# A convolution and SwiGLU kernel: bursts of the down projection one step later, the copy behind the product, and x and out on the software DMA queue

## The chip, the core and the metric

The kernel runs on one core of one Trainium2 chip. The metric is the device time of one execution in microseconds; the kernel before has a median of 895.02 us over 10 runs (894.46 to 896.08).

## The reference

x has 8 sequences of 4096 tokens with 192 channels. Stage one is a causal convolution with 7 taps: the 192 channels are 8 heads of 24, and each head has one softmax-normalised kernel of 7 weights. Stage two is a SwiGLU feed-forward block with an inner width of 1536 on the 32768 tokens that come out. All is in float32.

```python
w = softmax(weight, axis=-1)                       # 8 heads x 7 taps
x_pad = np.concatenate([zeros(B, 6, D), x], axis=1)
conv = np.einsum('hk,bskhg->bshg', w, windows(x_pad)).reshape(B * S, D)
g, v = conv @ moe_w_gate, conv @ moe_w_val         # 192 -> 1536
out = (g / (1 + np.exp(-g)) * v) @ moe_w_out       # 1536 -> 192
```

## The kernel before

The tokens are worked off in blocks of 512 (TB); two blocks make a unit of 1024 tokens (UB, UT), so there are 64 blocks and 32 units. The inner width is cut into 12 chunks of 128 (NCH). One pass of the main loop (L374) is a step g: one chunk of one block. A unit has 24 steps, and s is the step within its unit (L376).

In a step TensorE makes the gate product of chunk g and the value product of chunk g - 1 (emit_gv, L277), both over 192 channels in three pieces of 64 rows. The gate uses the upper half of the array's rows and the value the lower half, so the two run side by side. ScalarE puts SiLU on the gate (emit_silu, L292), and VectorE multiplies it with the value product from PSUM and writes h as fp16 (emit_h, L297). gate and val have two PSUM buffers each (ppool, L70); a val buffer is free again when its product h is made.

The down projection runs in bursts of three chunks (TR, L49): emit_f2 (L302) takes three chunks of h in two halves, in two successive steps out of three. F2_LAG (L50) says how many steps behind the gate it runs: 4. Behind the last burst of a block, emit_store (L337) copies the two accumulators to SBUF, one on ScalarE (L340), one on VectorE (L341); this stands ahead of emit_h in the step's order (L407 to L412). The 384 KB of a block go to `out` on SP's queue, four steps into the next block (L429).

The third step of three has no burst, and four of these eight gaps in a unit take the convolution of the next unit (emit_conv, L218, at s = 0, 3, 6, 9): small matmuls of band matrices (toep) with x as fp16, into two PSUM tiles. Since the two halves of the array swap banks between bursts, a relay stands between a burst and the next: a nop on GpSimd's queue that waits for the last matmul of a burst and that the first matmul of the next burst waits for (emit_relay, L209).

The convolved tokens have to be transposed. ScalarE copies them to SBUF as fp16 (emit_conv_out, L243, at s = 3, 4, 9, 10), GpSimd repeats the first 64 channels behind the others (emit_dup, L251), SP writes each block to DRAM (emit_to_dram, L257, at s = 11, 12), 57 partitions by 9 rows of 512 bytes, and SP reads it back by three transposing DMAs for each block (emit_transpose, L269, one a step from s = 16). The result xq of the first block of the next unit is needed by that unit's step 0, piece by piece.

x itself comes in on SP's queue as float32 (emit_fetch, L88, at s = 6 for the unit after the next: 64 x 9, 64 x 8 and 62 rows of 768 bytes), and GpSimd casts it in three parts (emit_x_cast, L104, at s = 14 to 16).

The order on all five engines is the written one (manual_schedule, L108): each engine works off its queue in the order in which the code emits, and waits only for data and buffers. Ahead of the main loop stand the loads (x of unit 0, all weights in two parts, x of unit 1, all on SP's queue), the making of the band matrices on VectorE, the convolution of unit 0, the casts of the weights in four parts, and the way through DRAM of blocks 0 and 1.

## Time and profile before

| What | Value |
|---|---|
| median of 10 runs | 895.02 us (894.46 to 896.08) |
| the profiled execution | 895.45 us |
| its span in the profile | 893.7 us, TensorE clock 0.999 |
| TensorE matmuls busy | 836.2 us (94%) |
| VectorE, ScalarE, GpSimd busy | 559.9, 547.8, 89.8 us |
| first gate matmul | 40.8 us |
| start of units 1, 3, 4 and 31 | 68.2, 121.56, 147.81 and 861.4 us |
| moved by DMA | 100.8 MB, 113 GB/s on average |
| issued by SP's queue | 63 out stores, 63 writes of xc, 189 transposes, 104 x loads |

The span is the time from the first to the last instruction; the execution's own time lies 1.75 us above it. In the profile PE stands for TensorE, PEld for its weight loads, DVE for VectorE, ACT for ScalarE, POOL for GpSimd and SPq for SP's queue, which issues DMAs. A row of the timeline has its start and its length in us; what stands in brackets at its end is the idle time of the engine before it and what ended that. In the list of waits, the numbers behind a pair are the sum in us, the count and the longest. A matmul's recorded length overlaps with the next one's, so steps are measured from start to start.

### The profile page before, as it was taken

The numbers are of one execution on the slowest core, as the hardware profiler recorded it, in microseconds if no ns is written. First come the engines' busy times: TensorE is split into PE (matmuls) and PEld (weight loads), VectorE is DVE, ScalarE is ACT, GpSimd is POOL, SyncE is SP. The second block draws the span as 40 slices with busy tenths as digits, with TensorE's granted clock in tenths as the row PEclk, the third lists the DMA queues.
The fourth block names the chain that finished last, engine by engine and source line by source line (L and its number), as shares of the span: only waits on it lengthen the run. The fifth ranks groups of instructions, "written<-read, shape, count | busy, mean of one in ns | idle before, by whom it ended". The sixth has DMA issues, their size and how long they took to land.

```text
span 893.7 us, 28535 instructions
## 1 busy us (share of the span) xinstructions
PE 836.2 (94%) x11764; PEld 595.5 (67%) x11764; DVE 559.9 (63%) x865; ACT 547.8 (61%) x970; POOL 89.8 (10%) x148
## 2 busy tenths in 40 slices
PE   1199999999999999999999999999999999999997
PEld 0176776677676677676667777667767667777764
DVE  5066666666666666666666666666666666666665
ACT  3166666666666666666656666666666666666654
POOL 2111011011001011001011101101100101110000
PEclk9999999999999999999999999999999999999999
DMA  9554665454565464555555456545556645555351
GB/s 180 108 108 98 124 130 115 98 124 100 118 124 125 89 130 103 112 125 128 110 107 118 96 125 127 123 94 123 114 105 125 132 102 111 122 101 120 86 95 37
DMA packets 211843, 100.80 MB, mean 113 GB/s; under 512 B 107056, under 2 KB 210944, under 8 KB 211712
## 3 DMA queue, kind: packets, MB, share of 16 engines
q1 hardware_dynamic: 209292, 98.12, 52.4%
q8 instruction: 92, 1.51, 0.7%
q10 hardware_dynamic: 2420, 0.85, 0.6%
q14 instruction: 39, 0.32, 0.1%
HBM read 31.79 MB, written 41.98 MB: 83 GB/s over the span
## 4 chain that ended last, share of the span: by engine, by line
PE 84%; DMA 7%; DVE 6%; SPq 2%; issue 1%; ACT 1%; DVEq 0%; POOLq 0%
PE acc L312 28%; PE val L284 26%; PE gate L284 24%; PE cps L233 5%; DMA xq<-xc 4%; DMA xc<-stage 3%; DVE h L299 2%; DVE o_sb L341 2%; SPq L273 1%; DVE band L180 1%; SPq L346 0%; DMA wraw<-in_weight_dram 0%; ACT stage L245 0%; ACT sig L294 0%; ACT toep L188 0%
## 5 line engine op out<-in xcount | busy, mean ns | idle before, releaser
L299 DVE TENSOR_TENSOR h<-sig,val 128x512 f16<-128x512 f16 x768 | 518.1, 687 | 271.0 <-PE val L284 233.1
L294 ACT ACTIVATE sig<-gate 128x512 f16<-128x512 f32 x768 | 458.8, 597 | 308.3 <-PE gate L284 186.5
L284 PE MATMUL gate<-xq,w_sb 64*128 64x512 f16 x2304 | 614.2, 377 | 26.8 <-DMA xq<-xc 26.4
L284 PE MATMUL val<-xq,w_sb 64*128 64x512 f16 x2304 | 608.2, 377 | 12.8 <-DVE h L299 12.5
L284 PEld LDWEIGHTS <-w_sb 64*128 64x128 f16 x4608 | 287.9, 94 | 176.3 <-issue 70.4
L312 PE MATMUL acc<-wo_sb,h 64*128 64x192 f16 x6120 | 402.5, 243 | 0.5 <-DVE h L299 0.5
L312 PEld LDWEIGHTS <-h 64*128 64x128 f16 x6120 | 328.6, 94 | 84.5 <-DVE h L299 1.0
L233 PE MATMUL cps<-x,toep 64*128 64x216 f16 x1024 | 82.9, 257 | 13.2 <-POOL x L106 12.0
L106 POOL CAST x<-x 128x576 f16<-128x576 f32 x96 | 62.9, 674 | 310.2 <-PE acc L312 298.1
L233 PEld LDWEIGHTS <-toep 64*128 64x128 f16 x1024 | 63.1, 95 | 32.3 <-DVE toep L187 10.1
L341 DVE COPY o_sb<-acc 128x384 f32<-128x384 f32 x64 | 35.7, 558 | 56.5 <-PE acc L312 55.9
L245 ACT ACTIVATE stage<-cps 128x432 f16<-128x432 f32 x128 | 67.1, 526 | 2.0 <-PE cps L233 2.0
L253 POOL COPY stage<-stage 128x576 f16<-128x576 f16 x32 | 21.4, 669 | 428.3 <-PE acc L312 398.2
L340 ACT COPY o_sb<-acc 128x384 f32<-128x384 f32 x64 | 30.7, 479 | 1.7 <-PE acc L328 1.7
L193 ACT CAST w_sb<-w_st 128x1152 f16<-128x1152 f32 x4 | 4.4, 1150 | 20.2 <-issue 20.1
L180 DVE COPY_PREDICATED band<-mask,whl 128x228 int32<-128x228 int32 x14 | 6.9, 495 | 0.4
L188 ACT COPY toep<-band 64x456 f16<-64x456 f16 x2 | 1.2, 578 | 7.0 <-DVE band L180 7.0
L194 POOL CAST wo_sb<-wo_st 128x576 f16<-128x576 f32 x4 | 2.6, 670 | 13.0 <-DMA wo_st<-in_moe_w_out_dram 13.0
L92 POOL MEMSET x<- 6x192 f32 x8 | 2.0, 248 | 1.3 <-PE cps L233 1.3
L158 ACT ACT_TABLE_LOAD x1 | 1.3, 1283 | 0.7 <-PEq L447 0.7
L158 ACT ACTIVATE wexp<-wexp 128x56 f32<-128x56 f32 x1 | 0.2, 249 | 2.1 <-DVE wexp L155 2.1
L328 PE MATMUL acc<-wo_sb,h 128*128 128x192 f16 x12 | 1.3, 248 | 0.1
(21 smaller groups left out, 8.2 us busy)
## 6 DMA issues: line engine op xcount, KB each, us to landing
out_dram<-o_sb SPq DMA_DIRECT2D x63, 384.0 KB
xc<-stage SPq DMA_DIRECT2D x63, 256.5 KB
x<-in_x_dram SPq DMA_DIRECT2D x40, 384.0 KB
x<-in_x_dram SPq DMA_DIRECT2D x24, 432.0 KB
xq<-xc SPq DMA_TRANSPOSE x189
x<-in_x_dram SPq DMA_DIRECT2D x32, 46.5 KB
w_st<-in_moe_w_gate_dram SPq DMA_DIRECT2D x2, 576.0 KB
wo_st<-in_moe_w_out_dram SPq DMA_DIRECT2D x2, 576.0 KB
```

The source lines that it names most:

```text
L106: nc.gpsimd.tensor_copy(x16s[u % 2][:, gs, :], x32s[u % 2][:, gs, :])
L180: nc.vector.copy_predicated(band_w[:, hs], masks[k].unsqueeze(1).to_broadcast([P, 4, G]), whl_w[:, hs, k : k + 1].to_broadcast([P, 4, G]),)
L233: mm = nc.tensor.matmul(conv["ps"][a][:, :, e, :], toep[lo : lo + Q, h, c, :], x16[lo : lo + Q, :, h * grp : (h + 1) * grp], start=(phase ...
L245: nc.scalar.mul(conv[u][:, :, d0 : d0 + 2 * grp], conv["ps"][a].rearrange("p g e d -> p g (e d)"), 1.0 / SCALE,)
L253: nc.gpsimd.tensor_copy(conv[u][:, :, D:XD], conv[u][:, :, 0:Q])
L273: queue.dma_start_transpose(out=xqs[b][:, q, :], in_=drs[b][0:TB, q * Q : q * Q + P])
L284: last_mm[0] = nc.tensor.matmul(ps, w_r[lo : lo + Q, q, ts(j, P)], xq[lo : lo + Q, q, :], start=(q == 0), stop=(q == NQ - 1),)
L294: nc.scalar.activation(sj, ps, AF.Silu)
L299: nc.vector.tensor_tensor(hj, sj, ps, op=ALU.mult)
L312: mm = nc.tensor.matmul(acc[a][:, i, :], hlist[j][lo : lo + Q, ts(2 * a + i, P)], wo_r[lo : lo + Q, j, :], start=(j == 0 and half == 0 and ...
L340: nc.scalar.copy(o_sb[:, 0:2, :], acc[0])
L341: nc.vector.tensor_copy(o_sb[:, 2:4, :], acc[1])
```

## The change

F2_LAG becomes 5, so each burst moves by one step, and h gets a tenth buffer. The convolution moves with the gaps, to s = 1, 4, 7, 10 (in unit 0 to s = 7, 10, 13, 16), and with it its copies, the repeat (dup) and the two writes to DRAM (s = 12, 13; in unit 0 s = 18, 19); the transposes start at s = 16 as before (in unit 0 at s = 18). The copy of the accumulators stands behind emit_h. The store to `out` goes to GpSimd's DMA queue, one step later, except for the last block's. The fetch of x is cut into its DMAs, which GpSimd's queue issues one a step from s = 10, the upper partitions first; the casts move to s = 19 to 21. At the start, x of unit 0 is loaded by SP (lower half of the partitions) and ScalarE's queue (upper half), the weights come in quarters, and the last quarter and x of unit 1 are issued behind the transposes of block 0. The last quarter's cast stands in step 6 of unit 0, and the casts of unit 1's x in its steps 4 to 6. The write and the transposes of block 0 go from ScalarE's queue to SP's.

```diff
@@ -47,7 +47,7 @@
     UT = UB * TB
     XD = D + Q
     TR = 3
-    F2_LAG = TR + 1
+    F2_LAG = TR + 2
     SCALE = 1024.0
 
     assert D == NQ * Q and NQ == 3 and UB == 2 and UG * G >= TB
@@ -85,21 +85,27 @@
             tensor=x_flat.tensor, offset=t * D, ap=[[D, rows], [G * D, n], [1, D]]
         )
 
-    def emit_fetch(u):
+    def fetches(u, lower=nc.gpsimd, upper=nc.gpsimd):
+
         x32 = x32s[u % 2]
         t0 = u * UT - pad
+        tb = t0 + TB
+        tl = tb + (UG - 1) * G
+        todo = [
+            (upper, x32[Q:P, 0 : UG - 1, :], windows(tb, Q, UG - 1)),
+            (upper, x32[Q : Q + last_rows, UG - 1, :], x_flat[tl : tl + last_rows, :]),
+        ]
         if u % upb == 0:
             nc.gpsimd.memset(x32[0:pad, 0, :], 0.0)
-            nc.sync.dma_start(out=x32[pad:Q, 0, :], in_=x_flat[t0 + pad : t0 + Q, :])
-            nc.sync.dma_start(out=x32[0:Q, 1:UG, :], in_=windows(t0 + G, Q, UG - 1))
+            todo.append((lower, x32[pad:Q, 0, :], x_flat[t0 + pad : t0 + Q, :]))
+            todo.append((lower, x32[0:Q, 1:UG, :], windows(t0 + G, Q, UG - 1)))
         else:
-            nc.sync.dma_start(out=x32[0:Q, :, :], in_=windows(t0, Q, UG))
-        tb = t0 + TB
-        nc.sync.dma_start(out=x32[Q:P, 0 : UG - 1, :], in_=windows(tb, Q, UG - 1))
-        tl = tb + (UG - 1) * G
-        nc.sync.dma_start(
-            out=x32[Q : Q + last_rows, UG - 1, :], in_=x_flat[tl : tl + last_rows, :]
-        )
+            todo.append((lower, x32[0:Q, :, :], windows(t0, Q, UG)))
+        return todo
+
+    def emit_fetch(todo):
+        queue, dst, src = todo.pop(0)
+        queue.dma_start(out=dst, in_=src)
 
     def emit_x_cast(u, i):
         gs = slice(i * UG // 3, (i + 1) * UG // 3)
@@ -113,7 +119,9 @@
     nc.sync.dma_start(
         out=wraw, in_=bass.AP(tensor=weight.tensor, offset=0, ap=[[0, P], [K, H], [1, K]])
     )
-    emit_fetch(0)
+    first = fetches(0, nc.sync, nc.scalar)
+    while first:
+        emit_fetch(first)
 
 
     w_st = wpool.tile([P, NQ, Dff], fp32, tag="w_st", name="w_st")
@@ -124,15 +132,17 @@
     wg_v = moe_w_gate.rearrange("(q p) f -> p q f", p=Q)
     wv_v = moe_w_val.rearrange("(q p) f -> p q f", p=Q)
     wo_v = moe_w_out.rearrange("(c p) d -> p c d", p=P)
-    for f in range(0, Dff, 2 * FS):
-        fs = slice(f, f + 2 * FS)
-        cs = slice(f // P, (f + 2 * FS) // P)
+
+    def emit_weight_load(i):
+        fs = slice(i * FS, (i + 1) * FS)
+        cs = slice(i * FS // P, (i + 1) * FS // P)
         nc.sync.dma_start(out=w_st[0:Q, :, fs], in_=wg_v[:, :, fs])
         nc.sync.dma_start(out=w_st[Q:P, 0 : NQ - 1, fs], in_=wv_v[:, 1:NQ, fs])
         nc.sync.dma_start(out=w_st[Q:P, NQ - 1, fs], in_=wv_v[:, 0, fs])
         nc.sync.dma_start(out=wo_st[:, cs, :], in_=wo_v[:, cs, :])
-    if n_units > 1:
-        emit_fetch(1)
+
+    for i in range(3):
+        emit_weight_load(i)
 
 
     diag = const_pool.tile([P, G], i32, tag="diag", name="diag")
@@ -254,11 +264,11 @@
 
     drs = {}
 
-    def emit_to_dram(b, queue=nc.sync):
+    def emit_to_dram(b):
 
         u, i = divmod(b, UB)
         dr = tc.dram_tile([UG * G, XD], fp16, name=f"xc{b}")
-        queue.dma_start(
+        nc.sync.dma_start(
             out=dr.rearrange("(g r) d -> r g d", r=G),
             in_=conv[u][i * Q : i * Q + G],
         )
@@ -266,11 +276,11 @@
 
     xqs = {}
 
-    def emit_transpose(b, q, queue=nc.sync):
+    def emit_transpose(b, q):
 
         if q == 0:
             xqs[b] = xpool.tile([P, NQ, TB], fp16, tag="xq", name="xq")
-        queue.dma_start_transpose(
+        nc.sync.dma_start_transpose(
             out=xqs[b][:, q, :], in_=drs[b][0:TB, q * Q : q * Q + P]
         )
 
@@ -295,7 +305,7 @@
         return sj
 
     def emit_h(sj, ps, hlist):
-        hj = hpool.tile([P, TB], fp16, tag="h", name="h", bufs=9)
+        hj = hpool.tile([P, TB], fp16, tag="h", name="h", bufs=10)
         nc.vector.tensor_tensor(hj, sj, ps, op=ALU.mult)
         hlist.append(hj)
 
@@ -343,7 +353,7 @@
         if b == n_blocks - 1:
             nc.scalar.dma_start(out=o_v[:, 0:2], in_=o_sb[:, 0:2])
             return lambda: nc.sync.dma_start(out=o_v[:, 2:4], in_=o_sb[:, 2:4])
-        return lambda: nc.sync.dma_start(out=o_v, in_=o_sb)
+        return lambda: nc.gpsimd.dma_start(out=o_v, in_=o_sb)
 
     for fill in range(2):
         for phase in range(2):
@@ -353,19 +363,19 @@
             emit_conv_out(0, fill, a)
         if fill == 0:
             emit_dup(0)
+    emit_to_dram(0)
     emit_weight_cast(0)
-    emit_to_dram(0, nc.scalar)
     emit_weight_cast(1)
     for q in range(NQ):
-        emit_transpose(0, q, nc.scalar)
+        emit_transpose(0, q)
+    first = fetches(1, nc.sync, nc.sync) if n_units > 1 else []
+    while first:
+        emit_fetch(first)
+    emit_weight_load(3)
+    emit_weight_cast(2)
     emit_to_dram(1)
-    for i in range(2, 4):
-        emit_weight_cast(i)
     for q in range(NQ):
         emit_transpose(1, q)
-    if n_units > 1:
-        for i in range(3):
-            emit_x_cast(1, i)
 
     hlists, accs, stores = {}, {}, []
     ns = NCH * UB
@@ -399,34 +409,43 @@
             if half < 2 and not tail:
                 emit_f2(half, range(t * TR, (t + 1) * TR), accs[fb], hlists[fb])
                 burst = True
-        if more and s in (0, 3, 6, 9):
-            emit_conv(u + 1, s // 6, s // 3 % 2)
+
+        c0 = 7 if u == 0 else 1
+        if more and s in range(c0, c0 + 12, 3):
+            emit_conv(u + 1, (s - c0) // 6, (s - c0) // 3 % 2)
             burst = True
-        if burst and live:
+        if burst:
             emit_relay()
+        if val is not None:
+            emit_h(sil.pop(g - 1), val[0], hlists[vb])
         if g >= F2_LAG and fj == NCH - 2:
             if tail:
                 emit_f2_full(range(t * TR, NCH), accs[fb], hlists[fb])
             stores.append(emit_store(fb, accs.pop(fb)))
-        if val is not None:
-            emit_h(sil.pop(g - 1), val[0], hlists[vb])
         if g >= F2_LAG and fj == NCH - 1:
             del hlists[fb], xqs[fb]
         if more:
-            if s in (3, 4, 9, 10):
-                emit_conv_out(u + 1, s // 6, s % 3)
-            if s == 5:
+            if s in (c0 + 3, c0 + 4, c0 + 9, c0 + 10):
+                emit_conv_out(u + 1, (s - c0) // 6, (s - c0) % 3)
+            if s == c0 + 5:
                 emit_dup(u + 1)
+            if u == 0 and 4 <= s < 7:
+                emit_x_cast(1, s - 4)
             if u + 2 < n_units:
-                if s == 6:
-                    emit_fetch(u + 2)
-                if 14 <= s < 17:
-                    emit_x_cast(u + 2, s - 14)
-            if s in (11, 12):
-                emit_to_dram((u + 1) * UB + s - 11)
-            if 16 <= s < 16 + UB * NQ:
-                emit_transpose((u + 1) * UB + (s - 16) // NQ, (s - 16) % NQ)
-        if s % NCH == 4 and stores or not live:
+                if s == 10:
+                    todo = fetches(u + 2)
+                if 10 <= s < 14 and todo:
+                    emit_fetch(todo)
+                if 19 <= s < 22:
+                    emit_x_cast(u + 2, s - 19)
+            if s in (c0 + 11, c0 + 12):
+                emit_to_dram((u + 1) * UB + s - c0 - 11)
+            t0 = 18 if u == 0 else 16
+            if t0 <= s < t0 + UB * NQ:
+                emit_transpose((u + 1) * UB + (s - t0) // NQ, (s - t0) % NQ)
+        if u == 0 and s == 6:
+            emit_weight_cast(3)
+        if s % NCH == 5 and stores or not live:
             for st in stores:
                 st()
             stores.clear()
```

## Prediction

> **What bounds the kernel now.** I read the page's busy shares and its chain first, then the groups, then one unit (24 steps, two blocks) in the timeline, then SP's queue and the waits.

> ```profile
> PE 836.2 (94%) x11764; PEld 595.5 (67%) x11764; DVE 559.9 (63%) x865; ACT 547.8 (61%) x970; POOL 89.8 (10%) x148
> PE 84%; DMA 7%; DVE 6%; SPq 2%; issue 1%; ACT 1%; DVEq 0%; POOLq 0%
> L341 DVE COPY o_sb<-acc 128x384 f32<-128x384 f32 x64 | 35.7, 558 | 56.5 <-PE acc L312 55.9
> ```

> TensorE is the bound, with two admixtures: VectorE (6% of the chain) and the way of the convolved tokens through DRAM (DMA 7%, SPq 2%). The third line is VectorE idling 0.9 us before each accumulator copy. One such copy, with the product behind it and the matmul that waits for that:

> ```profile
> 112.09 0.56 DVE L341 COPY o_sb<-acc 128x384 f32<-128x384 f32 x1 [0.92 <-PE acc L312]
> 112.56 1.28 DVE L299 TENSOR_TENSOR h<-sig,val 128x512 f16<-128x512 f16 x2
> 113.29 0.37 PE L284 MATMUL val<-xq,w_sb 64*128 64x512 f16 x1 [0.38 <-DVE h L299]
> ```

> The starts of each step's first gate matmul give the step lengths: 1.14 us with a burst, 1.02 with a convolution, 0.65 with neither. 16 x 1.14 + 4 x 1.02 + 4 x 0.65 = 24.92 us would be a unit; units take 26.24 (121.56 to 147.81). The other 1.32 us follow the two copies: 0.56 and 0.19 where val waits, 0.24 twice where the two halves of the array realign, 0.08 where a burst waits for a fresh h.

> The second limit lies in SP's queue. A unit's tokens are written to DRAM (L261) and read back transposed (L273) before the next unit can start:

> ```profile
> 108.36 2.95 SPq L261 DMA_DIRECT2D xc<-stage  x2
> 114.25 1.84 SPq L273 DMA_TRANSPOSE xq<-xc  x1
> 116.20 0.51 SPq L346 DMA_DIRECT2D out_dram<-o_sb  x1
> 116.77 7.22 SPq L273 DMA_TRANSPOSE xq<-xc  x5
> ```

> ```profile
> SPq L273 <- DMA xc<-stage: 98.5, 32, 9.6
> ```

> ```profile
> PE gate L284 <- DMA xq<-xc: 26.4, 7, 23.7
> ```

> By the completion events the first write, issued at 108.36, is complete at 114.17 and the third transpose of the block at 120.89, 12.54 us after that issue. The next unit starts at 121.56 and needs this piece 0.43 later, at 122.00: only 1.1 us are left, and at several unit starts nothing (the last line, the first one apart).

> ```profile
> 109.00:114.00 5.00, 4.62 (x60) 2.78 (x58) 3.46 (x6) 2.88 (x7) 1.28 (x2) 1.00 0.21 61
> 126.00:131.00 5.00, 4.99 (x75) 3.88 (x73) 3.40 (x6) 3.54 (x7) 0.67 (x1) 1.00 0.88 225
> ```

> These are stretches of the write and of an x fetch; the last two columns are DMA share and GB/s. The write keeps 0.21 of sixteen engines busy, about three, and moves 61 GB/s; the fetch uses them all. So the two 513-packet writes go one after the other through three engines (126 packets per us, 0.0238 us each on its engine: 4.07 us a write).

> [...]from 31 to 35 us, 512-byte packets of ACT's queue and 768-byte packets of SP's each pass at 35 per us on two shared engines, one pair in 57 ns, hence 33 ns for the 768-byte one. Software DMA is in no run here[...]. [...]one relay ran at 685.63 while a copy ran from 685.12 to 685.79.

> **The change, part by part.**

> *Bursts one step later, product ahead of the copy.* The product no longer waits 0.9 us plus 0.56 us. The copy moves behind it: burst end to copy end grows to about 0.9 us, and the next block's first burst is 1.3 us after the burst's end, so it fits (0.03 us at worst). The burst reads an h that is one step older. All 1.32 us per unit go: a unit of pure TensorE work is 24.92. What is late next is the write-and-transpose chain.

> *Convolution one step later.* It must fill another gap, so its last copy-out ends later. In the kernel before, that is 1.93 us into step 10, at 13.04 of 26.24. Afterwards it is 1.93 into step 11, which starts at 7 x 1.14 + 4 x 1.02 = 12.06: 13.99 of 24.92. The chain had 13.20 us to the unit's end and now has 10.93. Taking the output store out of SP's queue gives back its slot (116.14 to 116.77, 0.63): chain 11.91. The third piece lands at 25.90 and is wanted at 24.92 + 0.43 = 25.35: a stall of 0.55, period 25.47.

> *x fetch on the software queue.* It moves from step 6, after which the engines were nearly quiet when the write began, to steps 10, 11 and 12, behind relays at 12.06, 13.20 and 14.34. [...]Each of the three engines carries 1/16 of the fetch: of the first part's 32 packets about 8 are left, about 4 of the second[...], and 36 of the third: 48 x 0.033 = 1.6 us, all ahead of the write's end[...]. Bounds: 0 if the packets slip into gaps[...]; I take 1.8.

> *Store on the software queue.* Issued at step 17, behind the relay at 19.07[...]. 32 packets x 0.033 = 1.05[...]. Bounds 0 and 1.05; I take 0.5.[...]

> Period: 25.47 + 1.8 + 0.5 = 27.8, against 26.24 undisturbed and (861.4 - 68.2)/30 = 26.44 on average.

> *Start.* A quarter of the weights and unit 1's x move behind the first block. About 3.5 MB stand ahead of its write, at 0.2 MB per us from 2.8 us: to 20.4; write 4.1 + 1.0, three transposes 1.25 apart and 2.65 to land: the third piece at 30.6 instead of 41.7. But 1.7 MB then come ahead of the second block's write: to 39, landed about 44, third transpose 49.3, wanted at step 12, about 45.5: 3.8 us stall. Unit 1's convolution ends in step 17 of unit 0 (about 54.4 + 1.93), and its chain, now with the second write between transposes, takes some 13.2: 69.5, where it was 69.47. The gain is given back: 0, bounds -8 and +5.

> *End.* Unit 31 has no convolution and loses its stalls: 22.3 + 6.9 = 29.2 instead of 32.25.

> Sum: 69.5 - 0.43 + 29 x 27.8 + 26.0 (unit 30, no fetch) + 29.2 = 930.5 of span. The profiled execution took 895.45 for a span of 893.7 and lies 0.43 above the median: 930.5 + 1.75 - 0.43 = **932**.

> **Rivals.**

> *The chain stays nearly clear (faster).* If write packets pass among fetch packets almost free, as the fetch alone needs 55 ns per packet and engine of which 33 are engine time, the period is 25.5 to 26.0: 864 to 879. For it: this is the removal of a stall seen 63 times. Against it: the write alone fills its three engines, so every foreign packet pushes it. It decides while fetch and store together cost under 1.05 us per unit (98.3 + 30 x 26.52 + 1.3 = 895).

> [...]A relay must pass within 0.64 + 0.48 + 0.64 = 1.76 us of the one before. [...]Against it: the relay at 685.63.

> *Nothing to be seen.* The two effects cancel, period 26.5: 895.

> **Chances.** Chain with contention 0.65 (own range 900 to 955), chain clear 0.22, relays held 0.10, cancelled 0.03. About 0.2% (1.8 us) is what a measurement can tell from no change. Faster 0.22, same 0.03, slower 0.75. The range 872 to 962 leaves out half of the clear case, half of the held relays and the tail of the first.

> **What would show it.** Right: VectorE's 0.9 us ahead of L341's copy gone, val's waits for h gone, and at every unit start a gate matmul waiting 2 to 3 us for xq; the write taking about 7.5 us instead of 5.82; first gate near 28. Wrong: units near 25 us with no gate wait, or bursts waiting on GpSimd. The prediction fails first if the writes meet no other packets on their engines.

## The result, and the profile after

The changed kernel takes **1025.42 us** (median of 8 runs, 1022.18 to 1027.48), the kernel before 895.36 us (median of 29, 893.92 to 896.42): ratio 1.1452, 95% interval 1.1443 to 1.1462. The change costs 130 us; 932 was forecast, a loss of 37. The profiled execution took 1025.11 us with a span of 1023.2.

From the page of the kernel after: engines, chain, two groups of instructions.

```profile
PE 870.6 (85%) x11764; PEld 580.2 (57%) x11764; DVE 563.5 (55%) x865; ACT 547.7 (54%) x970; POOL 201.7 (20%) x308
...
PE 73%; DMA 20%; SPq 5%; issue 1%; POOL 0%; ACT 0%; DVE 0%; POOLq 0%
...
L294 PE MATMUL gate<-xq,w_sb 64*128 64x512 f16 x2304 | 641.6, 392 | 129.1 <-DMA xq<-xc 127.5
...
L351 DVE COPY o_sb<-acc 128x384 f32<-128x384 f32 x64 | 35.3, 551 | 0.8 <-PE acc L338 0.8
```

VectorE has left the chain (6% before), and its idle time ahead of the accumulator copy is 0.8 us in all, where it was 56.5: the first half of the change does what it says. DMA and SP's queue now hold 25% of the chain (9% before). Note that TensorE is busy for 34 us *longer* with the same 11764 matmuls, and that the mean gate matmul takes 392 ns instead of 377: some of them ran slower.

The waits of the same kernel (sum in us, count, longest):

```profile
PE gate L294 <- DMA xq<-xc: 127.5, 73, 9.3
PEld L294 <- DMA xq<-xc: 110.0, 32, 4.8
...
PEld L322 <- POOLq L221: 8.6, 16, 0.9
```

The gate's wait for xq was 26.4 us in 7 waits; it now comes at every unit start. No wait of val for h is left in the list. Step lengths by the starts of the gate matmuls, medians over units 2 to 30, say the same: steps 2 to 22 are 1.14, 1.02 and 0.65 us to the digit, but step 23 is 4.30 (1.14 without a wait), step 0 2.47 (1.14) and step 1 1.92 (1.02). The units take 30.51 us on average, before 26.42.

One unit boundary in the timeline of the kernel after (start, length, what; in brackets idle time before it), first GpSimd, then SP's queue, then TensorE:

```profile
487.31 0.71 POOL L108 DMA_DIRECT2D x<-in_x_dram  x1 [0.26 <-POOL x L99]
488.42 0.55 POOL L108 DMA_DIRECT2D x<-in_x_dram  x1 [0.40 <-PE val L294]
489.55 1.25 POOL L108 DMA_DIRECT2D x<-in_x_dram  x2 [0.57 <-PE acc L322]
494.36 0.79 POOL L356 DMA_DIRECT2D out_dram<-o_sb  x1 [3.56 <-PE val L294]
497.50 1.90 POOL L112 CAST x<-x 128x576 f16<-128x576 f32 x3 [2.35 <-DMA x<-in_x_dram]
...
488.41 4.09 SPq L271 DMA_DIRECT2D xc<-stage  x2
497.21 8.35 SPq L283 DMA_TRANSPOSE xq<-xc  x6
...
497.57 0.67 PE L322 MATMUL acc<-wo_sb,h 64*128 64x192 f16 x12 [0.34 <-POOLq L221]
...
499.37 0.66 PE L322 MATMUL acc<-wo_sb,h 64*128 64x192 f16 x12
502.43 0.39 PE L294 MATMUL gate<-xq,w_sb 64*128 64x512 f16 x1 [2.40 <-DMA xq<-xc]
...
503.06 0.37 PE L294 MATMUL gate<-xq,w_sb 64*128 64x512 f16 x1 [0.23 <-DMA xq<-xc]
...
503.65 0.58 PE L294 MATMUL gate<-xq,w_sb 64*128 64x512 f16 x1 [0.20 <-DMA xq<-xc]
...
504.03 1.19 PE L322 MATMUL acc<-wo_sb,h 64*128 64x192 f16 x12
504.99 0.63 PE L294 MATMUL gate<-xq,w_sb 64*128 64x512 f16 x1
...
507.25 0.38 PE L294 MATMUL gate<-xq,w_sb 64*128 64x512 f16 x1
```

The first write goes out at 488.41, between the fetch's DMAs. By its completion event it is done at 497.16, 8.75 us later (5.83 before), and the transposes, which wait for it, begin at 497.21. The gate then stands for 2.40 us and waits twice more, for the second and third piece. And look at what follows: the matmuls after the wait take 0.63 us instead of 0.38 and are issued 0.43 apart instead of 0.21, until about 507. The windows of this boundary name the reason (busy time of each engine, granted clock, DMA share, GB/s):

```profile
500.60:504.00 3.40, 1.13 (x6) 0.33 (x8) 0.00 (x0) 0.00 (x0) 0.00 (x0) 0.95 0.66 135
504.00:507.40 3.40, 3.40 (x32) 2.44 (x30) 1.38 (x2) 1.19 (x2) 0.00 (x0) 0.55 0.36 77
507.40:510.80 3.40, 3.40 (x56) 2.36 (x52) 2.36 (x4) 2.25 (x5) 0.00 (x0) 1.00 0.02 5
```

In the 3.4 us after the wait TensorE had 0.55 of its clock and made 32 matmuls; in the next 3.4 us, 56. The clock records show 31 such stretches, 28 of them 3.413 us long, 116 us in all (3 us before).

The records show more. The starts of all 31 stretches lie whole multiples of 3.413 us apart. If one cuts the kernel after into such intervals, from 60 us on, then each of the 29 that were followed by half clock had at most 1.46 us of TensorE matmuls in it, and each of the 220 at full clock that were not had at least 1.73. What happens between these two figures this run does not show.

### The profile page after: what moved, and what is told of

It is laid out like the page before. It is cut to its first block, busy times and chain, and to the rows that moved or that the text cites. A ratio compares the mean times of both kernels' runs of the same rounds, so it can differ in the third digit from the quotient of the medians.

```text
span 1023.2 us, 28609 instructions
## 1 busy us (share of the span) xinstructions
PE 870.6 (85%) x11764; PEld 580.2 (57%) x11764; DVE 563.5 (55%) x865; ACT 547.7 (54%) x970; POOL 201.7 (20%) x308
## 4 chain that ended last, share of the span: by engine, by line
PE 73%; DMA 20%; SPq 5%; issue 1%; POOL 0%; ACT 0%; DVE 0%; POOLq 0%
PE gate L294 42%; PE acc L322 23%; DMA xq<-xc 12%; PE cps L243 5%; DMA x<-in_x_dram 5%; SPq L283 4%; PE val L294 3%; DMA xc<-stage 2%; DMA w_st<-in_moe_w_val_dram 1%; POOL x L108 0%; SPq L108 0%; SPq L139 0%; SPq L140 0%; SPq L142 0%; PE acc L338 0%
## 5 line engine op out<-in xcount | busy, mean ns | idle before, releaser
L294 PE MATMUL gate<-xq,w_sb 64*128 64x512 f16 x2304 | 641.6, 392 | 129.1 <-DMA xq<-xc 127.5
L294 PE MATMUL val<-xq,w_sb 64*128 64x512 f16 x2304 | 642.1, 392 | 0.0
L294 PEld LDWEIGHTS <-w_sb 64*128 64x128 f16 x4608 | 247.5, 97 | 271.4 <-DMA xq<-xc 110.0
L322 PE MATMUL acc<-wo_sb,h 64*128 64x192 f16 x6120 | 357.3, 249 | 2.3 <-POOLq L221 2.2
L322 PEld LDWEIGHTS <-h 64*128 64x128 f16 x6120 | 290.2, 96 | 113.9 <-POOLq L221 8.6
L356 POOL DMA_DIRECT2D out_dram<-o_sb x63 | 49.0, 777 | 571.0 <-PE val L294 571.0
L243 PE MATMUL cps<-x,toep 64*128 64x216 f16 x1024 | 79.6, 276 | 17.0 <-POOL x L112 16.0
L243 PEld LDWEIGHTS <-toep 64*128 64x128 f16 x1024 | 59.6, 105 | 53.1 <-issue 20.1
L108 POOL DMA_DIRECT2D x<-in_x_dram x97 | 64.1, 662 | 122.3 <-PE val L294 93.6
```

The costliest lines, as they stand in the source:

```text
L108: queue.dma_start(out=dst, in_=src)
L243: mm = nc.tensor.matmul(conv["ps"][a][:, :, e, :], toep[lo : lo + Q, h, c, :], x16[lo : lo + Q, :, h * grp : (h + 1) * grp], start=(phase ...
L294: last_mm[0] = nc.tensor.matmul(ps, w_r[lo : lo + Q, q, ts(j, P)], xq[lo : lo + Q, q, :], start=(q == 0), stop=(q == NQ - 1),)
L322: mm = nc.tensor.matmul(acc[a][:, i, :], hlist[j][lo : lo + Q, ts(2 * a + i, P)], wo_r[lo : lo + Q, j, :], start=(j == 0 and half == 0 and ...
L356: return lambda: nc.gpsimd.dma_start(out=o_v, in_=o_sb)
```

## Experiments

All medians are over units 2 to 30, in us: the write from issue to completion, the third piece's landing after that, the two together (the chain), and the time at half clock in the whole run. The times of the kernels before and after, of "before, software queue", "before, split write", "the same, other start" and "split, queues as before" are medians of four executions or more; the others are single executions. The kernel after varies by 5 us, so nothing is read from differences of that size between single executions.

| Kernel | time | unit, mean | write | third piece | chain | half clock |
|---|---|---|---|---|---|---|
| before | 895.4 | 26.42 | 5.83 | 7.32 | 13.14 | 3 |
| after | 1025.4 | 30.51 | 8.59 | 6.78 | 15.33 | 116 |
| fetch by ScalarE's queue | 1029.5 | 30.72 | 8.40 | 6.82 | 15.62 | 119 |
| fetch early | 929.3 | 27.35 | 5.79 | 7.32 | 13.17 | 41 |
| filler matmuls | 992.6 | 29.52 | 8.63 | 6.77 | 15.68 | 20 |
| queues as before | 934.0 | 27.60 | 5.81 | 7.60 | 13.41 | 37 |
| before, software queue | 906.3 | 26.79 | 5.79 | 7.21 | 13.04 | 5 |
| store by SP | 1038.0 | 31.00 | 8.56 | 7.28 | 15.76 | 133 |
| split write | 849.2 | 25.09 | 4.02 | 6.97 | 10.91 | 10 |
| before, split write | 884.4 | 26.27 | 2.91 | 6.92 | 9.84 | 4 |
| convolution earlier | 883.8 | 25.70 | 7.56 | 7.37 | 14.95 | 19 |
| split and fetch early | 846.7 | 25.01 | 2.87 | 6.95 | 9.90 | 5 |
| the same, other start | 846.6 | 25.04 | 2.88 | 7.03 | 9.94 | 9 |
| split, queues as before | 845.3 | 24.95 | 2.89 | 7.09 | 10.07 | 10 |

**Does the meeting of fetch and write make the loss?** The changed kernel with the fetch six steps earlier:

```diff
-                if s == 10:
+                if s == 4:
                     todo = fetches(u + 2)
-                if 10 <= s < 14 and todo:
+                if 4 <= s < 8 and todo:
```

> The changed kernel with one edit: the fetch stays on the software queue but is issued in steps 4 to 7 instead of 10 to 13, so that it is over before the write begins. Theory (the fetch beside the write, on the same three engines): the write is back at about 6 us, the stall at a unit start at 0.5 to 1 us, the clock stays up, a unit takes 25.5 to 26.2 us: 870 to 895 us. Rival (the software queue itself[...]): no change, over 1000 us. Rival (the convolution's later place alone makes the stall): over 950 us.

929.3 us: 96 us of the 130 are gone, and the write is back at 5.79. So the meeting is the cause of most of the loss. The time lies above the theory's range and below that of the last rival: the boundaries still stall, because the chain is 13.17 long and not 11.91 as in the prediction.

**Is it the size of the packets on the software queue?** The fetch in its new place, but by ScalarE's hardware queue:

```diff
-                    todo = fetches(u + 2)
+                    todo = fetches(u + 2, nc.scalar, nc.scalar)
```

> The changed kernel with one edit: the fetch of x in the main loop is issued by ScalarE's hardware DMA queue instead of GpSimd's software queue, in the same steps 10 to 13. Theory (packet size: the software queue packs the fetch into packets of 4608 bytes[...]): with 768-byte packets the write takes about 7.6 us instead of 8.75, the stall at each unit start shrinks by 1.1 us or more[...]: 945 to 995 us. Rival (only the bytes beside the write count): 1015 to 1030. Rival (GpSimd's queue holds the relays): the waits for relays go, and the time falls by 10 us at most.

1029.5 us, as in the rival that only the bytes count; the theory of this run fell. The queues on the page (packets, MB, share of 16 engines), first of the kernel after:

```profile
q0 software_dynamic: 14960, 51.25, 17.7%
```

and with the fetch on ScalarE's queue, q10:

```profile
q10 hardware_dynamic: 36356, 27.11, 10.3%
q0 software_dynamic: 7056, 24.78, 7.2%
```

The software queue makes packets of 3.4 KB on average, the hardware queue 0.75 KB. The write was lengthened alike: by 2.76 and 2.57 us. So neither the size of the packets nor the queue that sends them explains the longer write. What fits is the number of bytes that pass on the engines during it; they are counted below, where the prediction is gone through. The page also gives the mean length of a packet's record: 10.3% of 16 x 1027.7 us over 36356 is 47 ns.

**Is the half clock a cost of its own?** 28 small matmuls ahead of step 23, into a PSUM tile that nobody reads; they keep TensorE busy where it would wait. The kernel does all of the reference's work and this besides. (The matmuls themselves stand in emit_fill, left out here.)

```diff
+        if more and s == 23:
+            emit_fill(u)
```

> The changed kernel with 28 small matmuls added in front of step 23 of each unit (about 2.5 us of work on one half of the array into a PSUM tile that nobody reads); nothing else is changed and all of the reference's work is done. Theory (about 1.7 us of each unit's length is TensorE at half clock after its idle time at the unit's start): the added work falls into the idle time, the clock stays up or drops later, steps 1 and 2 go back to 1.02 and 1.14 us: 970 to 1005 us, less than without it. Rival (steps 0 to 2 are long because they wait for data): 1020 us or more.

992.6 us: 33 less, though work was added. Span and granted clock of the kernel after,

```profile
core 0: 1023.2 us, clock 0.945
```

and with the filler:

```profile
core 0: 990.8 us, clock 0.991
```

The write is as long as before this edit (8.63); step 1 is back at 1.02. The write goes out 14.75 us after the unit's first gate instead of 16.37. So the half clock costs the kernel after at least 33 us: it delays the convolution, and with it the next write.

**The first half of the change alone** (bursts, copy, convolution and the new start): fetch in step 6 and stores, both on SP's queue.

```diff
-                if s == 10:
-                    todo = fetches(u + 2)
-                if 10 <= s < 14 and todo:
-                    emit_fetch(todo)
+                if s == 6:
+                    todo = fetches(u + 2, nc.sync, nc.sync)
+                    while todo:
+                        emit_fetch(todo)
...
-        return lambda: nc.gpsimd.dma_start(out=o_v, in_=o_sb)
+        return lambda: nc.sync.dma_start(out=o_v, in_=o_sb)
```

> The changed kernel with the queues of before: the fetch at step 6 on SP's queue, the stores on SP's queue; bursts, copy, place of the convolution and start as changed. Theory (the chain of write and transposes, 13.1 us, starts at 13.99 of a unit of 24.92): each unit start waits about 1.8 us, a unit takes 26.7 us, the clock stays up: 895 to 925 us. Rival (the first half of the change is a gain and only the software queue loses it): under 875 us.

934.0 us, above the range: the first half loses 39 us by itself. Its waits:

```profile
PE gate L294 <- DMA xq<-xc: 82.2, 49, 9.3
...
PEld L294 <- DMA xq<-xc: 9.2, 8, 3.5
```

The convolution stands one step later and the chain is 13.41 long, so the third piece is late at every unit start (step 0 takes 3.19 us). That eats the gain of 1.3 us per unit and more.

**The second half alone:** the kernel before, fetch and stores on GpSimd's queue, in their old steps.

```diff
-                    emit_fetch(u + 2)
+                    emit_fetch(u + 2, nc.gpsimd)
...
-        return lambda: nc.sync.dma_start(out=o_v, in_=o_sb)
+        return lambda: nc.gpsimd.dma_start(out=o_v, in_=o_sb)
```

> The kernel before with the second half of the change alone: the fetch of x in the main loop and the stores of out are issued by GpSimd's software queue, in their old steps (6, and 4 and 16). Theory (only a fetch that meets the write of the convolved tokens costs): the fetch is over before the write begins at 13 us of a unit, units stay at 26.2 us: 885 to 905 us. Rival (the software queue costs by itself[...]): over 930 us.

906.25 us (905.47 to 907.23), ratio 1.0124, interval 1.0107 to 1.0141; just above the range. The write keeps its 5.79; what is new is in the list of waits, which has neither line in the kernel before:

```profile
PEld L312 <- POOLq L211: 16.3, 30, 1.2
...
PE acc L312 <- POOLq L211: 4.5, 9, 0.7
```

L211 is the relay. The three DMAs of step 6 stand next to each other in GpSimd's queue, the relay of step 7 behind them, and step 8 takes 1.35 us instead of 1.14 (medians); all 39 waits stand in it. So DMAs on GpSimd's queue did hold relays here: the units grow by 0.37 us, 11 us in all. This is what the prediction's second rival feared, the relays held; one such DMA takes GpSimd 0.55 to 0.79 us. The relay at 685.63 that the prediction cites ran beside a copy; behind three of these DMAs in a row relays waited. In the kernel after, with one DMA in a step, such waits come to 0.5 us in steps 10 to 14. Its list has 8.6 and 2.2 us of waits for a relay, but most stand in step 21, where the relay is behind a cast of x that waits for x to land.

**The store alone back on SP's queue**, in the changed kernel (the last two lines of the diff above).

> The changed kernel with its stores of out issued by SP's queue instead of GpSimd's, in the same step. Theory (the fetch's packets on the three engines of the write and the half clock make the loss, the store is a minor share): 1010 to 1032 us, write still 8 us or more. Rival (the store's packets on the software queue hold the transposes, as the fetch's hold the write): 960 to 1005, with third transposes landing a microsecond or more sooner after the write's completion than 6.78 us.

1038.0 us, 6 above the range of the theory and far from the rival's. The third piece lands 0.5 us later (7.28), so in this place SP's queue is the worse one, and putting the store back regains nothing of the loss.

**Is the root that the write runs on three engines?** Each write of the changed kernel in two DMAs, 48 rows and 9 rows.

```diff
-        nc.sync.dma_start(
-            out=dr.rearrange("(g r) d -> r g d", r=G),
-            in_=conv[u][i * Q : i * Q + G],
-        )
+        rows = dr.rearrange("(g r) d -> r g d", r=G)
+        nc.sync.dma_start(out=rows[0:48], in_=conv[u][i * Q : i * Q + 48])
+        nc.sync.dma_start(out=rows[48:G], in_=conv[u][i * Q + 48 : i * Q + G])
```

> The changed kernel with one edit: each write of 57 rows to DRAM is two DMAs, 48 rows and 9 rows. Theory[...]: the write is complete in about 3 us instead of 8.75 although the fetch runs beside it, no stall at the unit starts, a unit takes about 25 us: 850 to 875 us. Rival (the fetch's volume or the writing to DRAM sets the write's time, not the number of engines): over 990 us.

849.2 us, just under the range, and 176 less by this edit alone. The page's engines and chain:

```profile
PE 810.7 (96%) x11764; PEld 560.7 (66%) x11764; DVE 563.2 (66%) x865; ACT 547.4 (65%) x970; POOL 203.0 (24%) x308
...
PE 88%; DMA 7%; SPq 3%; issue 1%; POOL 0%; ACT 0%; DVE 0%; POOLq 0%; ACTq 0%
```

and its waits:

```profile
PE gate L293 <- DMA xq<-xc: 15.0, 11, 6.7
```

The median unit is 24.94 us, every step at its undisturbed length in the median. All but 1.9 of the 15.0 us that remain lie at the start. The fetch still meets the write (4.02 us here, 2.9 where they do not meet), but the chain is 4.4 us shorter. A write that meets nothing takes 2.91 us as two DMAs, against 5.83 as one of 57 rows, which kept 0.21 of the sixteen engines busy. That the split write runs on more of them is an estimate from these two times; its engines are not shown.

The same edit in the kernel before (there with `queue` in place of `nc.sync`):

> The kernel before with each write of 57 rows as two DMAs of 48 and 9 rows, nothing else. Theory (before, the copy's stall sets a unit and the chain only now and then): units stay at 26.24 us, the waits at unit starts go (about 5 us in all) and the first block comes some us sooner: 878 to 892 us. Rival (the chain sets the units already in the kernel before): units under 25.5 us, below 875 us.

884.37 us (883.66 to 884.79), ratio 0.9878, interval 0.9863 to 0.9892. Its waits:

```profile
PE gate L283 <- DMA xq<-xc: 17.6, 2, 16.8
...
PE val L283 <- DVE h L298: 12.5, 33, 0.4
```

The boundary waits are gone and the first gate comes at 33.9 us instead of 40.8, but val's wait for h stays to the tenth, and the median unit with it (26.25). So each edit removes its own limit: the split alone gains 11 us, the first half of the change alone loses 39, and the two together gain 50 (the last run below).

**Can the chain be kept clear without the split?** The changed kernel with the fetch in steps 4 to 7 and the convolution three steps earlier (the first of its four at step 22 of the unit before), transposes from step 14; the lines for the fetch and the transposes are left out here.

```diff
-        c0 = 7 if u == 0 else 1
+        c0 = 7 if u == 0 else -2
+        if s == 22 and u + 2 < n_units:
+            emit_conv(u + 2, 0, 0)
+            burst = True
```

> The changed kernel with the fetch in steps 4 to 7 (as in the run with the early fetch) and the whole convolution one gap earlier: steps 22 of the unit before, 1, 4 and 7, and with it the copies, the repeat, the write (steps 9, 10) and the transposes (from step 14). The write stays one DMA of 57 rows. Theory (the write starts too late in the unit): the chain starts 3.3 us earlier and fits, no stall at unit starts but the first, 24.95 us a unit: 850 to 870 us. Rival (the slow write or the pace of the transposes costs wherever it stands): over 890 us.

883.8 us: neither range holds it, though it is 11.5 under the kernel before. Most unit starts are clear (the median of step 0 is 1.14), although the write takes 7.56 us among the fetch's packets: with three steps more, its length no longer shows. The list of waits tells what was missed:

```profile
PE gate L294 <- DMA xq<-xc: 31.2, 18, 10.2
PE cps L243 <- POOL x L112: 23.9, 32, 15.4
```

The convolution in step 22 now waits for the cast of x, which stands in steps 19 to 21 (0.4 us per unit: step 22 takes 1.44, where a step with a convolution takes 1.02), and unit 1's third piece is used at 79.2 us, still later than in the changed kernel (76.6).

**The best version.** Split write and early fetch, the start as changed:

> The changed kernel with each write of 57 rows as 48 and 9 rows and the fetch in steps 4 to 7; the start is left as it is. Theory: 843 to 852 us, units of 24.92 to 25.1 with the write at about 3 us, since it no longer meets the fetch; the start as in the split kernel, unit 1 at 58 us. Rival (the fetch was hidden already): 848 to 852 with the same unit mean of 25.09 as the split alone.

846.7 us, in the theory's range; the write takes 2.87 us, so it meets nothing now. The same with another start (in unit 0 both writes first, then the six transposes in steps 19 and 20):

> The changed kernel with each write of 57 rows as 48 and 9 rows, the fetch in steps 4 to 7, and in unit 0 both writes ahead of the transposes, which then come three in step 19 and three in step 20. Theory (the write on three engines is the root; with it split only the two kinds of boundary disturbance of up to 0.2 us per unit and the start remain): 838 to 850 us, units of 24.92 to 25.1, unit 1 at 55 to 59 us. Rival (the fetch in steps 10 to 13 was hidden already in the split kernel, and the early transposes at the start stand ahead of other work): 849 to 856, no gain over the split alone.

846.63 us (844.78 to 847.45), **ratio 0.9456, interval 0.9438 to 0.9475**. The third piece of unit 1 is used at 61.4 us instead of 63.4, but unit 31 starts at 814.4 instead of 814.7: the edit of the start brings nothing that can be told. Last, the split write with both queues as before, which leaves out the second half of the change:

> The changed kernel with the two queues as before (fetch on SP's queue in step 6, stores on SP's queue) and each write as 48 and 9 rows: only the first half of the change and the split. Theory (the software queue buys nothing once the write is short; it only disturbs a relay now and then, 0.1 us per unit): 842 to 849 us, units of 24.92 to 24.98. Rival (moving the fetch and the stores off SP's queue is what lets the split kernel run clear): 855 to 880, with gate waits for xq at unit starts.

845.31 us (845.29 to 846.35), ratio 0.9445, interval 0.943 to 0.9461. From its page the chain, and from its list the gate's waits:

```profile
PE 92%; DMA 4%; SPq 2%; issue 0%; POOL 0%; ACT 0%; DVE 0%; POOLq 0%; ACTq 0%
```

```profile
PE gate L293 <- DMA xq<-xc: 12.9, 8, 6.7
```

The two intervals overlap. The software queue gains nothing over SP's once the write is short: all of the 50 us come from the first half of the change together with the split. 39 of them lie in units 1 to 30, where bursts, copy and split act (unit 1 starts at 59.5 us and unit 31 at 813.6, before at 68.2 and 861.4); 9 lie ahead of unit 1, where the new start counts too, and 2 at the end.

## Why the prediction was wrong

The sign and the places were right: the copy's stalls go, and the chain of write and transposes takes their place, lengthened by the fetch. 932 was 93 us short. The spans show where: unit 1 starts 2.0 us later than forecast, lasts 8.8 longer, units 2 to 30 together 80.3, the end 1.6; the sum is 92.7. The terms of the period, as the prediction put them:

| Term, us | predicted | measured |
|---|---|---|
| unit of pure TensorE work | 24.92 | 24.94 (split write) |
| write issued, after the unit's first gate | 13.99 | 16.37 |
| write | 5.81 + 1.8 = 7.6 | 8.59 |
| third piece after the write | 6.72 - 0.63 + 0.5 = 6.6 | 6.78 |
| third piece used, after the unit's first gate | 0.43 | 1.2 |
| period | 27.8 | 30.51 |

- *"All 1.32 us per unit go": right.* Shown in the kernel after by its steps, and by the split kernel's 24.94.
- *"Convolution one step later", written at 13.99: the step that failed.* It counted the unit as if TensorE ran at full clock behind the stall that the same prediction put at its start. The write goes out 2.4 us later. 0.8 of that comes from waiting for the pieces one by one: the third is used 1.2 us after the first instead of 0.43. This costs the period nothing, since the third piece may then also land later (the table's last row but one). The other 1.6 is the half clock, since the filler brings the write to 14.75. The trace has it at nearly every unit start from 100 us on, 28 times for 3.413 us. The prediction had no half clock in it. Priced by the filler, this is at least 33 us; by the 1.6 us in each of 29 units, 46.
- *"48 x 0.033 = 1.6", taken as 1.8: the second step that failed, right in kind but too small.* The write lost 2.76 us. More packets meet it than the prediction counted, and the DMA records tell how many. The prediction had the fetch issued 1.93 us before the write; how soon its data would flow no run had shown. It is issued 1.12 us before, and its first packet comes 1.42 us after that (medians), so in the median nothing of it has passed when the write is issued. All of the fetch, 72 times 768 bytes on each engine (the mean of sixteen, counted with the store on SP's queue), runs beside the write, not 48. That is 38 ns for each; with the hardware queue, where 68 such packets begin during the write, 2.57 us give 38 again, and with the earlier convolution, where 40 meet it, 1.73 us give 43. So the count was off more than the price of 33. The store's packets begin in the last 1.3 us of the write; they don't lengthen it, for without them (store by SP) it takes 8.56. The 1.0 us that were missing make 28 us over the units.
- *The chain of 12.54 us from one unit* stands for a median of 13.14. In the kernel after this hardly shows (6.6 against 6.78 for the transposes), but it is why the first half alone loses 39 us, and why the early fetch doesn't win.
- *The store's slot given back, 0.63, and the store on the software queue, 0.5: the right sign.* Together they were to shorten the transposes by 0.13. With the store by SP's queue the third piece lands 0.5 us later and the kernel takes some 12 us more; in the early fetch, with the software store, it still takes the 7.32 of before. What the software store costs by itself no run shows.
- *No relay held by GpSimd's DMAs, the opposite of the second rival: right for one DMA in a step,* 0.5 us of waits in steps 10 to 14 of the kernel after; wrong for three in a row, 11 us in the kernel before with that queue.
- *Start, 69.5: too early by 7.1.* The third piece of block 0 is used at 32.4 us (30.6 was forecast), that of block 1 lands at 52.4 (49.3), behind a write that took 10.4 us among the weights; unit 1's write goes out at 61.5 (56.3), and its chain takes 15.1 (13.2).

As for the rivals: the early fetch is the test of the clear chain without contention, and at 929 us it too loses, so that rival was wrong on its own ground and not only on contention. Not settled: how much of the 80 us is half clock and how much the longer write. Each feeds the other: the write's delay makes the wait, and the half clock that came after the wait delays the next write. By the estimates above the one is worth 33 to 46 us and the other directly about 28; the early fetch, which takes away the meeting alone, returns 96 us with both.

## What to carry to other kernels

Before moving anything, look at the DMA share in the window of the transfer that is late: 0.21 of sixteen engines for a write of 57 rows pointed to the right place here, and cutting it into 48 and 9 rows turned a loss of 15% into a gain of 5%. When a forecast puts a wait of TensorE at the start of every unit, add the half clock that came behind it here (3.413 us in nearly every unit, at least 33 us in all), and let it delay what starts the next chain. The write on about three engines grew here by 38 ns for each 768 bytes of the fetch that passed on an engine beside it, from the software queue and from ScalarE's alike; count such bytes from the moment at which each DMA is really issued.
